# Key columns shared by neighbouring blocks: copied by DMA instead of ScalarE, with a new order of all work

## The chip, the cores and the metric

The kernel runs on one core of a Trainium2 chip. A core has a matrix engine (TensorE, PE in the profile; its weight loads are listed apart as PEld), a vector engine (VectorE, DVE), an activation engine (ScalarE, ACT), a general engine (GpSimd, POOL) and a sync engine (SyncE, SP), which in this kernel issues every DMA. Each engine works through its own list of instructions in order and waits on semaphores that the others, or a DMA that has landed, count up. PE writes its sums to PSUM; ACT and DVE copy ("evict") them from there to the on-chip memory SBUF.

The metric is the device time of one execution in microseconds. Lower is better. Before the change it was 191.21 us (median of 3 runs, 190.81 to 193.04).

## What is computed

One transformer layer in bfloat16 over 2048 positions of width 448: a sliding, dilated attention with 16 heads of width 28, and a shift-mixing MLP, each behind layer norms.

```python
def _A_ref(x, wqkv, wo):                      # attention
    H = 16; Dh = D // H; W, dil = 8, 2
    qkv = (x @ wqkv).reshape(B, S, 3, H, Dh)
    q, k, v = qkv[0], qkv[1], qkv[2]
    idx = pos[:, None] - off[None, :]         # off = 0, 2, 4, ..., 14
    logits = einsum("bhsd,bhswd->bhsw", q, kg) * Dh ** -0.5   # kg: k gathered at idx
    logits = where(idx >= 0, logits, -1e9)
    o = einsum("bhsw,bhswd->bhsd", softmax(logits), vg)
    return o.reshape(B, S, D) @ wo

def _B_ref(x, w1, w2, w3, w4):                # MLP
    h = gelu(layernorm(x) @ w1)
    # its four column quarters shifted by +1, -1, +2, -2 positions -> hs
    x1 = x + hs @ w2
    return x1 + gelu(layernorm(x1) @ w3) @ w4

h = x + _A_ref(layernorm(x), A_wqkv, A_wo)
return h + _B_ref(layernorm(h), B_w1, B_w2, B_w3, B_w4)
```

Position s attends to the keys s, s-2, ..., s-14. So a group of positions needs the 14 keys before its first one; the kernel keeps 16 columns (`PADK`) for them.

## The kernel before

**Blocks and phases.** The 2048 positions are 16 tiles of 128, and four blocks of 512 (t = 0 to 3). A block goes through these phases; a number behind the name is the block (M1 is phase M of block 1):

- N1: statistics and normalisation of the input x, tile by tile (DVE, ACT).
- A1: the normalised tiles are transposed (on PE for blocks 0 and 1, by a transposing DMA for blocks 2 and 3), then multiplied with the q and k columns of `wqkv`. Three chunks of 128 columns of q go to `qT`, three of k to `kk[t]`. The last 64 columns of each (the "half" chunk) are computed from their own weight copy `wr_s` and go to `qT[..., 3]` and `kr[t]`.
- V: the v product, evicted to `vt`; then SP copies it with overlaps into `vw` by three or four DMAs (the vw loads).
- A2 and S: for each chunk, DVE multiplies queries by eight shifted views of the keys (the "qk products", 128x4096, the half chunk 128x2048); PE sums over the head's rows; then the softmax, a handful of 128x512 steps on DVE and ACT, and a product into `pb` that can be done by DVE or POOL. PE turns `pb`, and ACT or DVE copies it to `pt[t]`.
- A3 and O: DVE spreads the weights with a mask into `bd` (four "mask products" a block, 80x2048), PE multiplies by `vw`, the result is copied to `actT`; then the product with `wo`, in two pairs of tiles, evicted to `xin` with the residual.
- B1 and M: statistics and normalisation of that, a transposing DMA (lntm to actT), the w1 product, gelu into `gT`.

The MLP's second part goes in five units of 2, 4, 4, 4 and 2 tiles (u = 0 to 4): B2 (the shifted w2 product, statistics), T (normalisation, transposing DMA), W3 (the w3 product and gelu; W30 is unit 0's) and B3 (the w4 product, the final sum, the store).

**Keys shared by blocks.** `kk[t]` holds 512 key columns behind 16 columns of the block before; phase A1 of block t fills those first 16 of block t+1 with an ACT copy (128x48 elements, SBUF to SBUF). `kr[t]` holds the half chunk's keys in eight groups of 64 positions, four on partitions 0 to 63 and four on 64 to 127, each group behind its own 16 columns; these are the last 16 columns of the group before, which lies on the other half of the partitions. Phase A1 evicts the half chunk's two PSUM banks (X and Y) with four ACT or DVE copies and then, with three more ACT copies from the same banks, fills the 16-column parts: 64x64, 64x48 and, for the next block, 64x16 elements. Lines 696 to 707 do this.

**What sets the order.** Each operation is recorded in a list and gets a number in the order of its creation. `ORDER` is a sequence of all these numbers; cut by engine, it is the order of each engine's list. `OTHER` names the operations that run on their second engine (`copy` has ACT first and DVE second; the `pb` product has DVE first and POOL second). `arrange` walks through the sequence, assigns buffers, and adds waits: a transposing DMA waits for all plain DMAs that stand between it and the transposing DMA before, and for that one; a plain DMA behind a transposing one waits for it:

```python
if op.insts[0][0] == "dma_start_transpose":
    op.deps.update(turned + moved)
    turned, moved = [op], []
elif op.is_dma and not callable(op.chan):
    op.deps.update(turned)
    moved.append(op)
```

ACT loads its function table anew (`emit_engine`) when it goes from exp and ln to gelu and back.

**The loads.** `load_rows` loads a weight matrix in two DMAs of two row chunks each; both have all 128 partitions. The input loads keep the order in which the code lists them: x tiles 0, 1, then 2 and 3, the q and k columns of `wqkv` (operations 12 and 13, 896 columns), x tiles 4 and 5 (14), 6 and 7 (15), the v columns (16, 17), the rest. All instructions are emitted from one helper, so nearly every row of the profile names line 986 (984 and 981 are its neighbours); they are told apart by their tiles and shapes.

Of the kernel before, what the change touches and what calls it, by code (L numbers as in the profile page):

```python
# [48 lines left out]
"""  # L49
OTHER = """  # L50
92 102 187 188 381 493 499 502 505 549 550
# [229 lines left out]
def bass_sequential_preLN__sliding_local_dilated__mixer_s_mlp__prompt_kernel(  # L281
    nc, A_x, A_wqkv, A_wo, B_x, B_w1, B_w2, B_w3, B_w4, out,
):
    _, SEQ, D = A_x.shape
# [26 lines left out]
    with ExitStack() as es:  # L311
# [118 lines left out]

        S.tag = "load"
# [4 lines left out]
        load_rows("wqk", wqkv_s[:, :, 0:2 * D], A_wqkv, 0, 2 * D)  # L436
# [231 lines left out]
        def phase_A1(t):  # L668
# [26 lines left out]

            def last(b, lo, n):
                return b(lambda v: v[64:128, 0:256].rearrange("p (j n) -> p j n", j=4)[:, lo:lo + n, 64 - PADK:])

            duo(half(X, 0, True), half(Y, 64, False), ((0, 256),))
            for h, b in enumerate((X, Y)):  # L700
                copy(qT[64 * h:64 * h + 64, 3, now:now + 256], b(lambda v: v[0:64, 0:256]))
# [3 lines left out]
            if t + 1 < NST:  # L705
                copy(kr[t + 1][0:64, 0:1, 0:PADK], last(Y, 3, 1), False)
                copy(kk[t + 1][:, :, 0:PADK], kk[t][:, :, 512:KVW])
# [320 lines left out]
```

## Time and profile before

| what | value |
|---|---|
| median of 3 runs | 191.21 us (190.81 to 193.04) |
| the profiled execution, its own time | 191.6 us |
| its span from first to last instruction | 189.9 us |
| granted TensorE clock | 1.00 throughout |
| DMA | 17.96 MB, 39.7% of 16 engines' span |
| SP waits before transposing DMAs for vw loads | 11.8 us, in 4 waits |

The span is what the trace covers; the 1.7 us around it belong to the execution's time too. A group's row reads: line, engine, operation, written tile, read tiles, shape and count, then busy us in all, mean ns of one, and the idle time just before with what ended it. A row of the timeline reads: start, duration, engine, line, operation, tiles, shape, count, and in brackets the idle time before it with what ended it. A row of the chain of waits reads: start, duration, what. A row of DMA issues reads: tiles, engine, kind, count, size of one, and the median us from issue to landing. In a row by stretch stand the stretch, its length, the busy time and count of PE, PEld, DVE, ACT and POOL, the granted clock, the busy share of the DMA engines and their GB/s.

Where the time lies, by the 40 slices of the page (each 4.75 us; a digit is a tenth of busy time, 9 is 90% or more):

```
PE   6799999999988668999999999999999999999994
DVE  6799999999999999897795337673973024001322
ACT  3569999999998999977698677049167004740330
```

### The profile page before, as it was taken

What the parts mean: (1) busy time and instruction counts of PE and PEld (TensorE: products, weight loads), DVE (VectorE), ACT (ScalarE), POOL (GpSimd) and SP (SyncE); (2) the same over time, 40 slices, a digit from 0 to 9 for tenths busy, and PEclk for the clock granted to TensorE, in tenths of its full rate; (3) what the DMA queues carried; (4) which work ended last, traced back from release to release, by engine and by line L of the source; (5) the groups of instructions that cost most, each with busy time, mean ns of one, the idle gap of its engine ahead of it and who ended that gap; (6) DMA issues with size and microseconds to landing.
All of it is one profiled execution on the core that took longest, in us unless ns stands there. A gap on an engine that the chain in (4) does not pass through costs nothing.

```text
span 189.9 us, 5626 instructions
## 1 busy us (share of the span) xinstructions
PE 178.4 (94%) x2434; PEld 107.5 (57%) x2434; DVE 127.4 (67%) x226; ACT 126.5 (67%) x295; POOL 26.9 (14%) x62
## 2 busy tenths in 40 slices
PE   6799989999988668999999999999999999999994
PEld 2494334545443434486544666666545664699973
DVE  6799999999999999897795337673973024001322
ACT  3569999999998999977698677049167004740330
POOL 2340000000002100202910000008026304000000
DMA  5993065554961553663534200518008202300202
GB/s 138 358 281 85 16 112 128 114 131 102 308 202 28 96 114 93 136 159 88 114 66 85 53 3 0 106 34 183 4 0 91 23 0 77 79 3 0 74 28 73
DMA packets 33217, 17.96 MB, mean 95 GB/s; under 512 B 21944, under 2 KB 32680, under 8 KB 33192
## 3 DMA queue, kind: packets, MB, share of 16 engines
q1 hardware_dynamic: 33192, 17.60, 39.7%
q8 instruction: 19, 0.31, 0.7%
q14 instruction: 6, 0.05, 0.1%
HBM read 7.91 MB, written 1.84 MB: 51 GB/s over the span
## 4 chain that ended last, share of the span: by engine, by line
PE 62%; DVE 17%; ACT 11%; DMA 6%; SPq 1%; issue 1%
PE ps L986 62%; DVE qk_r L986 9%; ACT arena L986 3%; DMA xin<-in_A_x_dram 3%; DMA actT<-lntm 3%; DVE bd_r L986 3%; ACT lntm L986 3%; ACT actT L986 2%; ACT vt L986 2%; DVE lntm L986 1%; DVE mx L986 1%; DVE st L986 1%; SPq L986 1%; ACT xin L986 1%; DVE pb L986 1%
## 5 line engine op out<-in xcount | busy, mean ns | idle before, releaser
L986 PE MATMUL ps<-actT,arena 64*128 64x512 bf16 (+1 forms) x756 | 68.8, 329 | 1.3 <-ACT vt L986 1.0
L986 PEld LDWEIGHTS ps<-actT,arena 64*128 64x128 bf16 x756 | 38.6, 94 | 27.3 <-ACT vt L986 2.6
L986 ACT ACTIVATE h3T<-ps 128x512 bf16<-128x512 f32 (+1 forms) x70 | 31.1, 515 | 33.7 <-PE ps L986 33.0
L986 PE MATMUL ps<-arena,h3T 64*128 64x448 bf16 (+2 forms) x434 | 44.5, 343 | 0.0
L986 PEld LDWEIGHTS ps<-arena,h3T 64*128 64x128 bf16 (+1 forms) x434 | 31.2, 94 | 11.5 <-ACT h3T L986 0.2
L986 DVE SCALAR_TENSOR_TENSOR qk_r<-ps,mrs,arena 128x448 bf16<-128x448 f32 (+1 forms) x17 | 10.6, 652 | 40.3 <-PE ps L986 33.2
L986 ACT ACTIVATE arena<-ps 128x512 bf16<-128x512 f32 (+6 forms) x73 | 32.8, 495 | 5.2 <-PE ps L986 4.6
L986 DVE TENSOR_TENSOR qk_r<-arena 128x4096 bf16<-128x4096 bf16 (+1 forms) x16 | 31.9, 2016 | 0.3 <-ACT arena L986 0.3
L986 POOL TENSOR_TENSOR arena<-arena,xin 128x448 f32<-128x448 f32 x16 | 16.7, 1066 | 43.5 <-DVE lntm L986 43.5
L986 DVE TENSOR_TENSOR bd_r<-arena,bmask 80x2048 bf16<-80x2048 bf16 x16 | 19.1, 1216 | 0.2 <-ACT arena L986 0.2
L986 PE MATMUL ps<-actT,w_s 64*112 64x512 bf16 x112 | 13.6, 378 | 2.2 <-DMA actT<-lntm 2.2
L986 PE MATMUL ps<-wo_s,actT 64*128 64x448 bf16 x128 | 14.8, 350 | 0.8 <-issue 0.5
L986 PE MATMUL ps<-w_s,arena 64*128 64x448 bf16 (+1 forms) x128 | 13.9, 350 | 1.0 <-ACT arena L986 1.0
L986 DVE SCALAR_TENSOR_TENSOR arena<-xin,rs_y,ps 128x448 f32<-128x448 bf16 x16 | 10.3, 676 | 4.0 <-PE ps L986 3.9
L986 PE MATMUL ps<-arena,actT 64*128 64x448 bf16 x112 | 12.5, 350 | 0.1
L986 ACT ACTIVATE lntm<-xin,nm 128x448 bf16<-128x448 bf16 x16 | 10.6, 685 | 2.2 <-DVE nm L986 2.0
L986 ACT ACTIVATE rs_x<-mv,epsilon 128x4 f32<-128x4 f32 (+2 forms) x16 | 4.9, 306 | 10.7 <-DVE mv L986 10.5
L986 ACT ACTIVATE actT<-ps 128x512 bf16<-128x512 f32 (+2 forms) x18 | 10.9, 644 | 1.4 <-PE ps L986 1.2
L986 PEld LDWEIGHTS ps<-actT,w_s 64*112 64x112 bf16 x112 | 7.7, 127 | 7.2 <-ACT arena L986 1.6
L986 PEld LDWEIGHTS ps<-w_s,arena 64*128 64x128 bf16 (+1 forms) x128 | 7.2, 94 | 6.1 <-ACT arena L986 1.1
L986 DVE BATCH_NORM_STATS2 st<-xin 128x6 f32<-128x448 bf16 x16 | 9.1, 616 | 1.7 <-DMA xin<-in_A_x_dram 1.4
L986 PEld LDWEIGHTS ps<-wo_s,actT 64*128 64x128 bf16 x128 | 6.2, 94 | 6.0 <-issue 0.9
(72 smaller groups left out, 156.6 us busy)
## 6 DMA issues: line engine op xcount, KB each, us to landing
arena<-in_B_w_dram SPq DMA_DIRECT2D x2, 896.0 KB, 8.1
out_dram<-qk_r SPq DMA_DIRECT2D x15, 112.0 KB, 1.9
arena<-in_B_w_dram SPq DMA_DIRECT2D x2, 784.0 KB, 5.2
vw<-vt SPq DMA_DIRECT2D x4, 320.0 KB, 5.7
vw<-vt SPq DMA_DIRECT2D x4, 256.0 KB, 3.9
arena<-in_A_wqkv_dram SPq DMA_DIRECT2D x2, 448.0 KB, 4.6
xin<-in_A_x_dram SPq DMA_DIRECT2D x2, 448.0 KB, 8.5
xin<-in_A_x_dram SPq DMA_DIRECT2D x3, 224.0 KB, 6.0
```

The costliest lines, as they stand in the source:

```text
L986: inst = getattr(eng, meth)(**kw)
```

## The change

Three edits.

1. The 16-column parts are no longer written by ACT. Where the four copies stood, four DMAs stand, which copy from the `kr[t]` and `kk[t]` that the other evictions have written, on SP's queue: `kra` (64 partitions x 4 groups x 16 columns, 8 KB), `krb` (6 KB), `krc` (2 KB, into the next block) and `kkp` (12 KB, into the next block). Block 3 has only the first two: 14 DMAs in all. `last`, which read the PSUM banks, is gone.
2. The q and k weights are loaded by `load_qk` in two column halves (columns 0 to 255 of q and of k, then 256 to 447), each with two DMAs for q and two for k: eight DMAs in place of two. Operation numbers from 14 on are therefore six higher.
3. `ORDER` and `OTHER` are new. `ORDER` has 864 numbers in place of 858. In the old numbering, `OTHER` no longer names the copy of tile 1's transpose (92), the eviction of chunk 0 of k (102), the norm of tile 1 in B1 (187), one A3 copy of block 3 (499) and one norm of unit 0 (549), so these run on ACT; it names the eviction of the half chunk of q from bank Y (119) for DVE and the `pb` product of block 3 for POOL, and of the two `pt` copies of block 3 the first in place of the second.

```diff
+        def load_qk(lo, n):
+
+            for g in range(2):
+                load_rows("wqk%d%d" % (lo, g), wqkv_s[:, :, g * D + lo:g * D + lo + n], A_wqkv, g * D + lo, n)
...
-        load_rows("wqk", wqkv_s[:, :, 0:2 * D], A_wqkv, 0, 2 * D)
+        for lo, n in ((0, 256), (256, D - 256)):
+            load_qk(lo, n)
...
-            def last(b, lo, n):
-                return b(lambda v: v[64:128, 0:256].rearrange("p (j n) -> p j n", j=4)[:, lo:lo + n, 64 - PADK:])
...
-            copy(kr[t][64:128, :, 0:PADK], last(X, 0, 4), False)
-            copy(kr[t][0:64, 1:4, 0:PADK], last(Y, 0, 3), False)
+            dma("kra%d" % t, kr[t][64:128, :, 0:PADK], kr[t][0:64, :, 64:KW], 64 * 4 * PADK * 2)
+            dma("krb%d" % t, kr[t][0:64, 1:4, 0:PADK], kr[t][64:128, 0:3, 64:KW], 64 * 3 * PADK * 2)
             if t + 1 < NST:
-                copy(kr[t + 1][0:64, 0:1, 0:PADK], last(Y, 3, 1), False)
-                copy(kk[t + 1][:, :, 0:PADK], kk[t][:, :, 512:KVW])
+                dma("krc%d" % t, kr[t + 1][0:64, 0, 0:PADK], kr[t][64:128, 3, 64:KW], 64 * PADK * 2)
+                dma("kkp%d" % t, kk[t + 1][:, :, 0:PADK], kk[t][:, :, 512:KVW], 128 * 3 * PADK * 2)
```

`OTHER` in the diff (new numbers, six higher):

```diff
-92 102 187 188 381 493 499 502 505 549 550
+125 194 387 496 498 508 511 556
```

What of the new order the prediction speaks of, in the new numbers, as the operations follow each other on one engine:

- DVE, start: statistics of x tiles 0 to 3, their norms, then the statistics of tiles 4 to 7 (205, 207, 209, 211), the norms of block 1, the statistics of block 2, the first qk product of block 0 (143), the norms of block 2, and the other three qk products of block 0. Before, three of block 0's products stood ahead of block 2's norms.
- SP: ..., transposing DMA of block 2's A1 (338), w1's second half, vw loads and `kr` copies of blocks 0 and 1, transposing DMA of block 3's A1 (449), a vw load, `kkp` of block 1 (246), vw loads and `kr` copies up to block 2, w2, w3, vw loads, B1's transposing DMA of block 0 (196), the vw load of 256 KB for block 2 (370), B1's transposing DMA of block 1 (315), `krb` of block 3, the first half of w4, ... Before, the load between the two transposing DMAs of B1 was one of 48 KB (366 in the old numbers).
- PE from O1 on: both pairs of O1 in order as their halves of A3 come, the first score chunk of block 3, the turn of block 2's `pb`, M0, all four A3 groups of block 2 with unit 0 of B2 between them, O2 and M1 mixed, unit 1 of B2, then W30. Before, two A3 groups of block 2 and the second pair of O2 (403, 404) stood behind M1, and that pair amid W30 and the w4 product of unit 0; the last score chunk of block 3 (489) stood ahead of W30 and now stands behind it.

58 rows, old and new, of the table ORDER are left out of this document.

## The prediction

> **What bounds the kernel now.** I read the page first, then the chain of waits in order of time.
>
> ```profile
> span 189.9 us, 5626 instructions
> ```
> ```profile
> 67.10 5.92 DMA actT<-lntm
> ...
> 73.07 35.45 PE ps L986 x583
> ...
> 108.60 78.75 PE ps L986 x820
> ```
>
> From 73.07 to 187.35 us the chain is PE alone (35.45 + 78.75), with 0.08 us between: the matrix work left at 73.07 fixes the rest. So a change gains only by getting PE through its early work sooner, or loses by opening holes later. The busy times by stretch (PE, PEld, DVE, ACT, POOL; then granted clock, DMA share, GB/s) say what bounds the early part:
>
> ```profile
> 5.00:10.00 5.00, 3.84 (x48) 2.50 (x48) 4.05 (x12) 2.54 (x8) 2.19 (x14) 1.00 1.05 359
> ...
> 15.00:20.00 5.00, 5.00 (x52) 2.17 (x50) 5.00 (x8) 5.00 (x14) 0.00 (x0) 1.00 0.19 43
> ...
> 55.00:60.00 5.00, 3.80 (x66) 1.61 (x66) 4.93 (x9) 4.97 (x14) 0.00 (x0) 1.00 0.13 32
> ```
>
> DVE and ACT are full from 15 us on; PE pays at the end of the attention part. The timeline of PE shows its holes there, in brackets:
>
> ```profile
> 56.35 0.42 PE L986 MATMUL ps<-bd_r,vw 80*32 80x64 bf16 x32 [0.38 <-DVE bd_r L986]
> 57.08 0.55 PE L986 MATMUL ps<-wo_s,actT 64*128 64x448 bf16 x4 [0.32 <-ACT actT L986]
> 58.14 0.55 PE L986 MATMUL ps<-wo_s,actT 64*128 64x448 bf16 x4 [0.51 <-issue]
> 64.39 3.23 PE L986 MATMUL ps<-actT,w_s 64*112 64x512 bf16 x28 [1.53 <-DMA actT<-lntm]
> 68.38 0.42 PE L986 MATMUL ps<-bd_r,vw 80*32 80x64 bf16 x32 [0.41 <-ACT arena L986]
> 69.75 1.93 PE L986 MATMUL ps<-w_s,arena 64*128 64x448 bf16 x16 [0.96 <-ACT arena L986]
> 73.07 3.23 PE L986 MATMUL ps<-actT,w_s 64*112 64x512 bf16 x28 [0.63 <-DMA actT<-lntm]
> ```
>
> They sum to 4.74 us. The two longest matmul rows are M0 and M1 (the w1 product of blocks 0 and 1), each waiting for its transposing DMA, which waits for the normalisation in phase B1.
>
> **Part one: work taken off ACT and DVE.** The copies that become DMAs, and operations that change engine:
>
> ```profile
> L986 ACT ACTIVATE arena<-ps 64x64 bf16<-64x64 f32 x4 | 0.9, 220 | 1.7 <-PE ps L986 1.7
> L986 ACT ACTIVATE arena<-ps 64x48 bf16<-64x48 f32 x4 | 0.8, 201 | 0.0
> L986 ACT ACTIVATE arena<-arena 128x48 bf16<-128x48 bf16 x3 | 0.8, 261 | 0.0
> L986 ACT ACTIVATE arena<-ps 64x16 bf16<-64x16 f32 x3 | 0.5, 181 | 0.1
> L986 ACT ACTIVATE actT<-ps 128x512 bf16<-128x512 bf16 x3 | 1.6, 597 | 0.5 <-PE ps L986 0.5
> L986 ACT ACTIVATE arena<-ps 128x512 bf16<-128x512 f32 x23 | 13.0, 618 | 0.0
> L986 ACT ACTIVATE lntm<-xin,nmr,rs_y 128x512 bf16<-128x512 bf16 x2 | 1.5, 799 | 0.0
> L986 DVE COPY actT<-ps 128x512 bf16<-128x512 bf16 x1 | 0.4, 418 | 0.0
> L986 DVE CAST arena<-ps 128x512 bf16<-128x512 f32 x1 | 0.7, 657 | 0.0
> L986 DVE TENSOR_SCALAR lntm<-xin,nm,rs_y 128x512 bf16<-128x512 bf16 x14 | 5.1, 407 | 0.4 <-ACT rs_y L986 0.3
> L986 ACT ACTIVATE arena<-ps 64x256 bf16<-64x256 f32 x16 | 6.0, 375 | 0.3
> ```
>
> ACT loses 14 small copies: 0.9 + 0.8 + 0.8 + 0.5 = 3.0 us, all before 73 us. But OTHER changes too. Three operations that DVE ran in the first two blocks go back to ACT (597 + 618 + 799 ns = 2.0 us) and save DVE 418 + 657 + 407 = 1.48 us; one 64x256 eviction goes from ACT (0.38) to DVE, where no row shows it: between 0.33 (half the 128x512 CAST, 657 ns) and 0.66 (all of it), and I take 0.4, half its elements plus something fixed. Net in front: ACT -3.0 + 2.0 - 0.4 = -1.4 us, DVE -1.1 (-0.8 to -1.15). The other moves (one softmax product to POOL, two evictions back to ACT) are of block 3 or the MLP, under the full PE, and cost nothing unless PE runs dry.
>
> **Part two: the loads.** Two q/k loads become eight.
>
> ```profile
> 2.20 0.98 SPq L986 DMA_DIRECT2D arena<-in_A_wqkv_dram  x2
> 3.22 1.07 SPq L986 DMA_DIRECT2D xin<-in_A_x_dram  x2
> 9.27 2.21 DVE L986 BATCH_NORM_STATS2 st<-xin 128x6 f32<-128x448 bf16 x4 [0.91 <-DMA xin<-in_A_x_dram]
> ```
>
> One issue is 0.98/2 = 0.49 us, so six more push the next load, x of tiles 4 and 5, from 3.22 to 6.14. DVE already waits 0.91 us for it and has nothing else in its order. It was 6.0 us under way (3.22 to 9.27) while the DMA engines moved 359 GB/s: it stood in a bandwidth queue behind the same weights, so it need not land 2.9 us later. Ends: 0 and 2.9; I take 0.5, near the queued row. On the other side the first q/k piece needs only the first column half and its first two tiles are evicted earlier, about half a microsecond for PE, which is not the bound there. I count that at nothing and expect this start to eat DVE's saving: even at 25 us.
>
> **Part three: the new DMAs on SP.** 14 copies of 16 columns enter SP's queue, each behind an ACT eviction, and each is ahead of what follows there.
>
> ```profile
> vw<-vt SPq DMA_DIRECT2D x4, 256.0 KB, 3.9
> ...
> vw<-vt SPq DMA_DIRECT2D x4, 48.0 KB, 2.6
> ...
> out_dram<-qk_r SPq DMA_DIRECT2D x2, 56.0 KB, 1.5
> vw<-vt SPq DMA_DIRECT2D x3, 16.0 KB, 5.2
> ```
> ```profile
> L986 DVE TENSOR_TENSOR qk_r<-arena 128x4096 bf16<-128x4096 bf16 x12 | 27.1, 2282 | 0.3 <-ACT arena L986 0.3
> ...
> L986 DVE TENSOR_TENSOR bd_r<-arena,bmask 80x2048 bf16<-80x2048 bf16 x16 | 19.1, 1216 | 0.2 <-ACT arena L986 0.2
> ```
>
> The nearest in size land in 1.5 to 5.2 us; I take 2.6, SBUF to SBUF. Plain and transposing DMAs wait for each other in the plan, so a copy queued behind a transpose waits for it. Who waits is a DVE product. The copies for blocks 0, 1 and 3 have over 4 us of DVE work in between. The tightest is block 2's first 16 keys (246 in the new numbering): it stands behind block 3's transpose (449) and one vw load, and product 377 reads it. Between the norms that feed 449 and that product DVE's order holds one and a half qk products (2.28 each), four mask products (1.22) and five softmax steps (priced as the CAST, 0.66): 11.6 us. Against it stand the transpose (4.5 to 5.9, from 59.90 to 64.39 and from the chain), two issues (0.63 each, below) and 2.6 to land: 8.4 to 9.8. Landing in 5.2 makes 12.4 and a stall of 0.8. I take none.
>
> **Part four: the order.** Here the gain must come.
>
> ```profile
> 59.90 2.12 SPq L986 DMA_TRANSPOSE actT<-lntm  x1
> ...
> 64.27 0.63 SPq L986 DMA_DIRECT2D vw<-vt  x1
> ...
> 89.89 2.04 SPq L986 DMA_TRANSPOSE actT<-lntm  x1
> ```
> ```profile
> 81.95 5.19 PE L986 MATMUL ps<-actT,arena 64*128 64x256 bf16 x92
> 86.97 0.92 PE L986 MATMUL ps<-wo_s,actT 64*128 64x448 bf16 x8
> ...
> 94.41 10.09 PE L986 MATMUL ps<-actT,arena 64*128 64x512 bf16 x92
> ```
>
> M0's transpose (before: 59.90): ACT now has 13 of the copies (2.8 us) and a few evictions less ahead of the last norm, so it can leave at about 57; M0 then waits instead for O1 (56.35 to 58.14 show it begin), whose last mask product now stands behind two softmax steps and a norm (0.66 + 0.66 + 0.41 = 1.7 us). M0 starts near 62, not 64.39.
>
> M1's transpose (67.10): O1's pairs now finish one after the other, two of the four statistics early; the last norm ends about 65.7. But a 256 KB vw load is now queued between the two transposes where a 48 KB one was (64.27): it goes out as M0 starts, so it lands at 62 + 0.6 + 3.9 = 66.5. With 4.5 to 5.9 for the transpose, M1 starts near 71.6, 1.5 us earlier.
>
> From M1 to W30 (first w3 product) PE took 81.95 - 73.07 = 8.88 us. The new order has both late O2 sums in there (0.92 each) and three short groups (about 0.42 each) elsewhere: 8.88 + 1.84 - 1.26 = 9.5, plus 0.8 of waiting for M1's last gelu: W30 at 81.9. That is the old time with 1.84 - 0.42 = 1.4 us more work done. The next turn (89.89) then limits: W31 has 1.8 us less to hide it and the statistics end only about 1 us sooner, so I take 1.3 us to the end. The later order still interleaves w1, w3 and w4 products with every transpose; I count no new hole.
>
> **The sum.** Span 189.9 - 1.3 = 188.6. The profiled execution's own time was 191.6, 1.7 above its span, so 190.3; the median of the runs was 191.2, 0.4 below that, which makes 189.9.
>
> **Rivals.**
> *ACT was the bound.* If the 2.8 us freed on ACT pass through and all 4.74 us of holes close: 191.2 - 4.7 = 186.5. For: ACT at 4.97 of 5 from 55 to 60. Against: DVE is at 5.00 longer, and gains 1.1.
> *The x load comes late.* If tiles 4 and 5 keep their 6.0 us, they land at 12.2; every full DVE stretch moves by 2.9: 189.9 + 2.9 = 192.8, slower than before as soon as they land more than 1.3 us after 9.27. Against: 359 GB/s. The Trainium skill ("DMA: Bandwidth & Descriptors", Specifications) says that runs under 512 B fall short of line rate through read-modify-write; the second half's runs are 192 columns, 384 B, and no row here shows such a load. Were its 393 KB to take twice their time at 359 GB/s, my estimate by that page is 1.1 us more, 193.9.
> *SP becomes the bound.* In-order copies behind transposes keep DVE idle before a product in blocks 1 to 3. Two misses of 2.0 to 2.6 us give 189.9 + 4.6 = 194.5, and one more 196 to 197. For: SP has 20 issues more, and the mutual waits of copies and transposes. Deciding point: 246 landing after DVE reaches 377.
> *It does nothing.* The time earned at M1 is given back at W31's turn: 191.2.
>
> **How the numbers follow.** Forecast (188.5 to 190.9) 0.37; nothing 0.13; ACT bound 0.18; late x 0.14; SP 0.18. The range reaches from the first rival's 186.5 to 195.0, which takes in the late load and over half of the SP case. 2% (3.8 us) is about what a measurement of this kernel tells from no change: faster means under 187.4, slower over 195.0. Faster gets the ACT rival, 0.18; slower the larger half of the SP rival and a little of the late load, 0.17; the rest, 0.65, is within.
>
> **What would show it.** Right: no DVE idle from the x load above 1.5 us; the ACT groups 64x64, 64x48, 64x16 and 128x48 gone; M0's matmuls near 62, M1's near 71.6; PE holes between 55 and 75 of 3 to 3.5 us; the last chain PE alone from there. Wrong: a qk product whose releaser is a DMA into the arena; M1 at 73 or later; a PE hole before W30 or W31 longer than 1 us; or first statistics of block 1 after 10.6.

## The result: a little slower, and the profile after

| | before | changed |
|---|---|---|
| median (22 runs each, side by side) | 191.63 us | 192.30 us |
| ratio, 95% interval | | 1.0049 (1.0025 to 1.0073) |
| span of the profiled execution | 189.9 us | 190.8 us |
| M0, M1, W30 start at | 64.39, 73.07, 81.95 | 64.50, 73.29, 83.22 |
| PE busy, DVE, ACT, POOL (us) | 178.4, 127.4, 126.5, 26.9 | 180.0, 128.6, 123.3, 30.9 |

The change makes the kernel 0.5% slower. Some executions of either kernel run in a slower state; every ratio here leaves those out, so 1.0049 is not 192.30/191.63. Helper rows name line 989 now (986 before, others in the kernels of the experiments), 984 is ACT's table load. The chain of waits of the changed kernel (start, duration, what) no longer goes over to PE alone at M1:

```profile
67.87 5.37 DMA actT<-lntm
73.29 6.39 PE ps L989 x60
...
87.21 2.77 DVE lntm L989 x4
...
98.35 1.09 ACT h3T L989 x2
...
103.27 84.26 PE ps L989 x989
```

PE alone begins 30 us later than before (103.27; before 73.07): between M1 and there the chain runs through DVE's norms of unit 1 and ACT. PE's timeline shows the holes that are left, and a new one:

```profile
59.56 0.42 PE L989 MATMUL ps<-bd_r,vw 80*32 80x64 bf16 x32 [0.66 <-DVE bd_r L989]
60.71 0.93 PE L989 MATMUL ps<-wo_s,actT 64*128 64x448 bf16 x8 [0.73 <-ACT actT L989]
64.50 3.23 PE L989 MATMUL ps<-actT,w_s 64*112 64x512 bf16 x28 [0.52 <-ACT vt L989]
...
73.29 1.07 PE L989 MATMUL ps<-actT,w_s 64*112 64x512 bf16 x8 [0.58 <-DMA actT<-lntm]
83.22 5.53 PE L989 MATMUL ps<-actT,arena 64*128 64x256 bf16 x98 [0.21 <-DVE mv L989]
...
97.03 5.75 PE L989 MATMUL ps<-actT,arena 64*128 64x512 bf16 x48
103.26 2.58 PE L989 MATMUL ps<-actT,w_s 64*112 64x512 bf16 x22 [0.47 <-ACT h3T L989]
```

PE's holes between 55 and 75 us sum to 3.20 us (4.74 before). The row at 103.26 is M2's first part, behind W31; it waits 0.47 us, and from W30 to there 20.04 us pass, which p4 below does in 19.14. Before, PE had no hole there. The row names a gelu of ACT (h3T) as what ended the wait, but M2 also needs block 2's transposing DMA, and that came no sooner: it left at 98.78, SP's next DMA, which waits for it, went out at 103.14, and M2's first weight load started at 103.22. In p4 the three times are 97.52, 101.86 and 101.95, and M2 does not wait. DVE's timeline shows the start and this stage:

```profile
10.11 1.68 DVE L989 BATCH_NORM_STATS2 st<-xin 128x6 f32<-128x448 bf16 x3 [2.10 <-DMA xin<-in_A_x_dram]
...
16.83 2.26 DVE L989 TENSOR_TENSOR qk_r<-arena 128x4096 bf16<-128x4096 bf16 x1
...
87.21 2.77 DVE L989 TENSOR_SCALAR lntm<-arena,mv,rs_y 128x512 bf16<-128x512 f32 x4 [1.07 <-POOL rs_y L989]
...
96.65 2.10 DVE L989 TENSOR_SCALAR lntm<-xin,nm,rs_y 128x512 bf16<-128x512 bf16 x4 [0.65 <-ACT rs_y L989]
...
99.38 6.42 DVE L989 TENSOR_TENSOR bd_r<-arena,bmask 80x2048 bf16<-80x2048 bf16 x4
```

In the kernel before, the same norms of unit 1 and two of the mask products were

```profile
87.90 1.92 DVE L986 TENSOR_SCALAR lntm<-arena,mv,rs_y 128x512 bf16<-128x512 f32 x4 [1.14 <-POOL rs_y L986]
...
97.15 2.35 DVE L986 TENSOR_TENSOR bd_r<-arena,bmask 80x2048 bf16<-80x2048 bf16 x2
```

So two things stand out: DVE waits 2.10 us for the x of tiles 4 and 5 (0.91 before) and begins its first qk product at 16.83 (15.98); and the same DVE operations take longer in the stage of W31 (four norms 2.77 for 1.92, mask products 1.6 each for 1.2). It is single instructions that stretch: one of unit 1's four norms takes 1.40 us where the median is 0.54, one of block 2's four takes 1.12 where it is 0.41, and the transposing DMA of M2 waits for the latter. POOL's timeline tells what ran beside them:

```profile
87.29 1.04 POOL L989 TENSOR_TENSOR arena<-arena,xin 128x448 f32<-128x448 f32 x1
...
97.40 4.21 POOL L989 TENSOR_TENSOR arena<-arena,xin 128x448 f32<-128x448 f32 x3
```

These are the additions of unit 0's and unit 1's residual. One takes 1.04 us beside the norms and 1.40 beside the mask products (1.01 late in the kernel, where three take 3.02).

### The profile page after: what moved, and what is told of

The parts are those of the page before. It is cut to its first block, busy times and chain, and to the rows that moved or that the text cites. A ratio compares the mean times of both kernels' runs of the same rounds, so it can differ in the third digit from the quotient of the medians.

```text
span 190.8 us, 5638 instructions
## 1 busy us (share of the span) xinstructions
PE 180.0 (94%) x2434; PEld 100.1 (52%) x2434; DVE 128.6 (67%) x221; ACT 123.3 (65%) x283; POOL 30.9 (16%) x63
## 4 chain that ended last, share of the span: by engine, by line
PE 51%; DVE 24%; ACT 15%; DMA 5%; SPq 3%; issue 1%; POOL 1%
PE ps L989 51%; DVE qk_r L989 8%; ACT arena L989 4%; DVE bd_r L989 4%; DVE st L989 3%; DVE lntm L989 3%; DMA actT<-lntm 3%; SPq L989 3%; ACT lntm L989 3%; DMA xin<-in_A_x_dram 2%; DVE mx L989 2%; DVE arena L989 1%; ACT actT L989 1%; ACT xin L989 1%; ACT h3T L989 1%
## 5 line engine op out<-in xcount | busy, mean ns | idle before, releaser
L989 PEld LDWEIGHTS ps<-actT,arena 64*128 64x128 bf16 x756 | 37.6, 94 | 28.5 <-POOL arena L989 1.3
L989 ACT ACTIVATE arena<-ps 128x512 bf16<-128x512 f32 (+3 forms) x62 | 31.2, 551 | 5.1 <-PE ps L989 4.7
L989 PEld LDWEIGHTS ps<-arena,h3T 64*128 64x128 bf16 (+1 forms) x434 | 24.6, 94 | 17.1 <-PE ps L989 0.2
L989 POOL TENSOR_TENSOR arena<-arena,xin 128x448 f32<-128x448 f32 x16 | 18.5, 1180 | 35.3 <-DVE lntm L989 19.9
L989 DVE TENSOR_TENSOR bd_r<-arena,bmask 80x2048 bf16<-80x2048 bf16 x16 | 20.8, 1327 | 0.2 <-ACT arena L989 0.2
L989 ACT ACTIVATE actT<-ps 128x512 bf16<-128x512 f32 (+2 forms) x20 | 12.3, 640 | 5.0 <-PE ps L989 5.0
L989 PE MATMUL ps<-wo_s,actT 64*128 64x448 bf16 x128 | 14.3, 350 | 0.9 <-ACT actT L989 0.7
L989 POOL TENSOR_TENSOR pb<-ls,mx 128x512 bf16<-128x512 f32 x2 | 2.9, 1426 | 56.1 <-ACT mx L989 56.1
L989 PEld LDWEIGHTS ps<-w_s,arena 64*128 64x128 bf16 (+1 forms) x128 | 6.6, 95 | 6.3 <-PE ps L989 0.9
L989 DVE TENSOR_SCALAR lntm<-arena,mv,rs_y 128x512 bf16<-128x512 f32 x14 | 7.7, 602 | 2.8 <-POOL rs_y L989 2.2
```

The lines of the kernel that those rows point to most:

```text
L989: inst = getattr(eng, meth)(**kw)
```

## The experiments

Theories at the start: (T1) the loss is the late x at the start and the hole behind W31, and the copies by DMA are harmless; (T2) the copies by DMA and SP's queue are the cost; (T3) ACT, or DVE, was the only bound, so that relief of the other is worth nothing. Each kernel was compared with the kernel before on the same chip; a ratio is to that.

**l1: the two whole weight loads again.**

```diff
-        for lo, n in ((0, 256), (256, D - 256)):
-            load_qk(lo, n)
+        load_rows("wqk", wqkv_s[:, :, 0:2 * D], A_wqkv, 0, 2 * D)
```

> The changed kernel, with the q and k weights loaded in the two whole transfers of before; the searched order and the copies by DMA stay. My theory: the eight issues put the x of tiles 4 and 5 on their way 3.1 us later than before, and DVE and PE carry 0.75 us of it (first product of q and k at 16.83 instead of 15.98). Undone, this stage gains 0.6 to 0.9 us, and if the gain is kept to the end the ratio to before is 1.000 to 1.002 (1.005 for the whole change). The rival, that a stage later on takes the time whatever reaches it: the first product comes earlier, M0 and M1 do not, and the ratio stays at 1.004 to 1.006. A second rival, that the order was searched for the late weights: ratio over 1.006.

Ratio 0.9974 (0.9945 to 1.0004), span 189.7. DVE's and PE's timelines of l1:

```profile
8.67 1.68 DVE L995 BATCH_NORM_STATS2 st<-xin 128x6 f32<-128x448 bf16 x3 [0.66 <-DMA xin<-in_A_x_dram]
...
15.44 2.26 DVE L995 TENSOR_TENSOR qk_r<-arena 128x4096 bf16<-128x4096 bf16 x1
```
```profile
63.20 3.23 PE L995 MATMUL ps<-actT,w_s 64*112 64x512 bf16 x28 [0.35 <-DMA actT<-lntm]
...
102.20 2.58 PE L995 MATMUL ps<-actT,w_s 64*112 64x512 bf16 x22 [0.47 <-ACT h3T L995]
```

Against the changed kernel the first product moves by 1.39 us, M0 by 1.30, the hole behind W31 by 1.06, the span by 1.1: what the start loses arrives at the end nearly whole, more than my 0.75. The hole behind W31 stays, as it must if it has a cause of its own. The ratio lies below what I expected (1.000 to 1.002).

**h1: the old order behind W30.**

```diff
-ORDER: the new one, 864 numbers
+ORDER: its first 482 numbers, then the rest in the order of the kernel before
```

> The changed kernel up to the first product of W30, in its own order (482 operations); every operation behind it in the order that the kernel before gives it. My theory: the hole of about 1.0 us in W31 (103.26, waiting for a gelu of ACT) belongs to the new order of the back part, so it goes, and the ratio falls to 0.998 to 1.001. The rival, that ACT cannot serve W31 earlier whatever the order, since its work up to there (S3, B12 and two table loads) hangs on DVE: the hole stays under another name and the ratio stays at 1.003 to 1.006.

Block 3's `pb` product and two of its copies also go back to their engines of before. Ratio 1.0219 (1.0165 to 1.0272): neither. PE's timeline:

```profile
85.78 0.40 PE L996 MATMUL ps<-qk_r,zc 128*32 128x512 bf16 x4 [3.22 <-DVE qk_r L996]
```

The old order has block 3's last score chunk ahead of W30, and the new one's DVE has not made its product by then. The splice makes its own hole, and the run says nothing on the hole behind W31.

**c2 and c3: the copies back on ACT,** c2 with the eight loads, c3 with two.

```diff
-            dma("kra%d" % t, kr[t][64:128, :, 0:PADK], kr[t][0:64, :, 64:KW], 64 * 4 * PADK * 2)
+            copy(kr[t][64:128, :, 0:PADK], last(X, 0, 4), False)
```

(and the other three likewise)

> The changed kernel, its order and its two column halves kept, with the 14 copies done by ACT again, each right behind the eviction of the same bank. If ACT sets the front (worth 3.0 us of its time less the 0.2 to 0.4 us that issuing costs elsewhere), the ratio rises from 1.005 to 1.013 to 1.020. My theory, that DVE sets it and ACT has room there: under 0.5 us more, 1.004 to 1.008. The rival that the transfers hurt (a queue on SP, a late wait): below 1.003.

> The new order alone: two whole weight loads, and the 14 copies done by ACT right behind the eviction of their bank. If the three parts of the change add up (eight loads +0.75%, copies by DMA -0.55%, whole change +0.49%), the order alone gives 1.002 to 1.004. The rival, that the order was worth something only together with the copies by DMA, or the loads cost less without them: above 1.006 or below 1.000.

c2: 1.0104 (1.0069 to 1.0139), M0 at 65.57 and M1 at 74.12, 1.07 and 0.83 us later than in the changed kernel. c3: 1.0036 (1.0018 to 1.0053). So the copies by DMA are worth 0.0055 (c2 against the changed kernel) and 0.0062 (c3 against l1) of the time, about 1.1 us of the 3.0 us that ACT loses: between the two sides of c2's expectation. DVE's timeline of c2 shows how ACT's work reaches DVE:

```profile
32.41 1.38 DVE L999 TENSOR_SCALAR lntm<-xin,nm,rs_y 128x512 bf16<-128x512 bf16 x4 [0.35 <-ACT rs_y L999]
...
44.70 0.69 DVE L999 TENSOR_REDUCE mx<-ls 128x64 f32<-128x512 f32 x1 [0.60 <-ACT ls L999]
```

Up to M0, DVE's waits for ACT sum to 1.71 us in c2 and 0.64 in the changed kernel, and the difference is the 1.07 us by which M0 is late. Neither engine alone is the bound, each waits for the other for moments (T3 falls), and the copies earn their place (T2 falls for this order). c3 is the new order by itself: it costs 0.36% before the copies earn anything.

**n1: the kernel before with the eight loads.**

```diff
-        load_rows("wqk", wqkv_s[:, :, 0:2 * D], A_wqkv, 0, 2 * D)
+        for lo, n in ((0, 256), (256, D - 256)):
+            load_qk(lo, n)
```

> The kernel before, with its order and its copies on ACT; only the q and k weights come in eight loads. My theory: the x of tiles 4 and 5 comes 1.2 to 1.5 us later and everything behind it moves by that: ratio 1.005 to 1.008, first product of q and k at 17.0 to 17.5. The rival, that only the new order, which does all statistics of block 1 at once, is exposed to the late x: 0.999 to 1.003.

1.0023 (0.9991 to 1.0054): by the ratio the rival's, by the first product (17.11) the theory's. DVE's timeline:

```profile
9.79 2.20 DVE L999 BATCH_NORM_STATS2 st<-xin 128x6 f32<-128x448 bf16 x4 [1.75 <-DMA xin<-in_A_x_dram]
14.71 2.20 DVE L999 BATCH_NORM_STATS2 st<-xin 128x6 f32<-128x448 bf16 x4 [0.51 <-DMA xin<-in_A_x_dram]
17.11 4.46 DVE L999 TENSOR_TENSOR qk_r<-arena 128x4096 bf16<-128x4096 bf16 x2
```

The x comes 0.5 us later than before (9.79; before 9.27), DVE waits for a second load too, the first product is 1.13 us late; M0 then is 0.67 us late (65.06). The old order absorbs half of it; the new one next to none (l1: 1.39 us at the first product, 1.30 at M0).

**l2 and l3: x ahead of the second column halves,** tiles 4 and 5 in l2, 4 to 7 in l3.

```diff
-        for lo, n in ((0, 256), (256, D - 256)):
-            load_qk(lo, n)
+        load_qk(0, 256)
         load_x(4, 2)
+        load_qk(256, D - 256)
         load_x(6, 2)
```

> The changed kernel with its eight loads, but the x of tiles 4 and 5 issued behind the fourth of them, ahead of the second column halves. My theory (the x issued late is the cost, the halves themselves are not): x lands near 8.7 as with two loads, ratio 0.996 to 0.999. The rival, that the halves cost by themselves (runs of 384 and 512 bytes, second halves on which PE then waits): PE waits over 1.5 us for the half chunk's weights or the second halves, ratio 1.002 to 1.006.

> The changed kernel with its eight loads, the x of tiles 4 to 7 issued behind the fourth of them, ahead of the second column halves. With tiles 4 and 5 alone ahead, the wait moved to tile 6 (1.59 us at 10.68). My theory, that the wait is a matter of place in the queue: no wait of DVE for x above 0.5 us now, but the second halves come last, and PE waits for the half chunk's weights 2 us or more (1.61 with two tiles ahead); the first product of q and k at 15.0 to 16.3, ratio 0.998 to 1.003. The rival, that six more loads cost little and only the x was late: PE's wait stays under 1.7 us and the ratio falls to 0.995 to 0.998.

l2: 1.0028 (0.9985 to 1.0070), as the rival has it; l3: 1.0125 (1.0077 to 1.0173), slower than both of its theories. In l2 no wait for tiles 4 and 5 is left, but tile 6 is waited for, and PE for the second halves, by way of POOL, which copies the half chunk's weights; DVE's and PE's rows:

```profile
10.68 0.63 DVE L996 BATCH_NORM_STATS2 st<-xin 128x6 f32<-128x448 bf16 x1 [1.59 <-DMA xin<-in_A_x_dram]
```
```profile
10.46 4.32 PE L996 MATMUL ps<-actT,arena 64*128 64x256 bf16 x76 [1.61 <-POOL arena L996]
```

In l3 DVE waits 0.29 us for x, but PE 2.74 us, up to 11.52, for the half chunk's weights, and the first product starts at 18.85. Each place in the queue that one load gains another loses: what is late is the whole queue.

**l4: four loads with whole rows.**

```diff
-        for lo, n in ((0, 256), (256, D - 256)):
-            load_qk(lo, n)
+        load_qk(0, D)
```

> The changed kernel with four q and k loads: two for all columns of q, two for all columns of k (runs of 896 bytes in place of 512 and 384). From 4 to 10 us the DMA engines moved 235 GB/s in the changed kernel at a busy share of 0.91, and 340 at 1.04 with the two loads of before. If the short runs cost, the rate is over 300 GB/s here, the x of tiles 4 and 5 lands before 9.0, the first product of q and k starts at 15.2 to 15.8: ratio 0.995 to 0.999. If the number of issues costs, half of it is left: x at 9.2 to 9.6, first product at 16.0 to 16.4, ratio 1.000 to 1.003.

0.9994 (0.9964 to 1.0024). x of tiles 4 and 5 is issued at 4.25 (3.22 in l1, 6.29 in the changed kernel) and read at 9.35 (8.67, 10.11); the first product starts at 16.10, as the theory of issues has it. The rate recovers as the theory of short runs has it. The stretch from 4 to 10 us (busy times of PE, PEld, DVE, ACT, POOL, then clock, DMA share, GB/s) of the kernel before, the changed one and l4:

```profile
4.00:10.00 6.00, 4.84 (x50) 2.85 (x50) 4.86 (x14) 2.93 (x10) 2.19 (x14) 1.00 1.04 357
```
```profile
4.00:10.00 6.00, 5.01 (x42) 2.61 (x42) 3.57 (x12) 3.41 (x10) 1.05 (x5) 1.00 0.91 235
```
```profile
4.00:10.00 6.00, 5.14 (x44) 2.93 (x44) 4.34 (x14) 3.56 (x10) 1.21 (x5) 1.00 1.02 327
```

SP's rows show one limit: eight issues take 4.05 us, 0.506 each, for 128 KB in the first half and 96 KB in the second. 131 thousand bytes in 0.506 us are 259 GB/s, 98 thousand 194, and SP asks for no more while it issues them; before, the DMA engines moved 357:

```profile
2.20 4.05 SPq L989 DMA_DIRECT2D arena<-in_A_wqkv_dram  x8
6.29 0.98 SPq L989 DMA_DIRECT2D xin<-in_A_x_dram  x2
```

But that limit is the smaller part. Behind the last of the eight issues, from 6.25 to 9 us, the rate is still 228 GB/s at a busy share of 0.93 (before 348 at 1.04), though larger loads are queued by then. Over the whole stretch the busy share fell by an eighth (0.91 for 1.04) and the bytes by a third, so a busy engine moved fewer bytes too. The shorter runs fit that, but they were not tested alone: l4 lengthens the runs and doubles the bytes of an issue together.

**p1, p2, p3, p4: POOL's additions moved.** POOL's list and, in p2, DVE's, PE's and SP's places of the last score chunk (numbers of the kernel before; 551 is unit 0's second addition, 612, 614 and 615 are unit 1's, 607 is a power in unit 1's norms):

```diff
-l1:     552 607 185 551 490 88 414 614 615 612 304
+p1, p2: 552 551 607 185 490 88 414 614 615 612 304
+p3:     552 551 607 614 615 612 185 490 88 414 304
-DVE l1: 606 299 609 610 611 608 405 482 484
+DVE p2: 606 482 299 609 610 611 608 405 484
-PE l1:  582 583 483 584
+PE p2:  582 483 583 584
```

p4 is the changed kernel itself, eight loads included, with p3's list on POOL.

> The changed kernel with two whole weight loads (ratio 0.9974 by itself), and four residual additions of POOL moved: that of unit 0 behind the one ahead of it, three of unit 1 behind the last mask product of block 3. My theory: DVE runs slower beside a POOL addition (unit 1's norms 2.77 us for four where the kernel before shows 1.92; mask products 1.6 us each there, 1.22 elsewhere). With the additions away the norms take about 1.95 and the mask products about 1.25 each, and the hole behind W31 shrinks by 0.2 to 0.5 us: ratio 0.994 to 0.997. The rival, that their length comes from something else (their operands, the port of PSUM, ACT beside them): the same lengths and 0.997 to 0.999.

> As p1, and the last score chunk of block 3 earlier: its query-key product on DVE in the 1.07 us in which DVE waits for POOL ahead of unit 1's norms (87.21 in the changed kernel), its matmuls between the first and second half of unit 0's first w4 sum. My theory: ACT's list is what starts W31's gelus late (98.35), and the score chunk's softmax steps stand in it ahead of them; the chain of that softmax starts 1.0 to 1.4 us sooner, the hole behind W31 closes: ratio 0.991 to 0.994. The rival, that the statistics of block 2 in the same list or PE's own queue set it: 0.995 to 0.998, with the hole at the same place.

> As p1 (two whole weight loads, unit 0's addition early), but the three POOL additions of unit 1 now stand directly behind that unit's norms, in the 7 us in which POOL waits; in p1 nothing stood between them and the place where they ran before, so they ran there again (97.02 to 101.2), and DVE's mask products beside them still took 6.42 us for four. If POOL's additions slow DVE, the mask products fall to about 4.9 us for four and block 2's norms from 2.10 to about 1.4; M2 (waiting for its transposing DMA in p1) comes 0.5 to 0.8 us sooner behind W30: ratio 0.988 to 0.994. The rival, that the length of these products is their own: 6.4 us again, and p1's time.

> The changed kernel as it is, eight loads included; only POOL's residual additions of units 0 and 1 stand earlier in POOL's list, as in p3. My theory: those additions beside DVE's norms and mask products are what opens the hole behind W31 (1.0 us), so it goes, and the ratio falls from 1.005 to 0.998 to 1.001; the start stays late (first product of q and k at 16.8). The rival, that ACT's list or the table loads open the hole: it stays, 1.003 to 1.006.

Ratios: p1 0.9898 (0.9840 to 0.9957), p2 0.9966 (0.9935 to 0.9998), p3 0.9922 (0.9885 to 0.9959), p4 0.9959 (0.9933 to 0.9985). p1 and p4 are faster than their theories, p3 as its own, p2 as its rival. In p1 only unit 0's addition really moved. The norms beside it went back to 1.91 us; the hole behind W31 stayed, now in the name of a transposing DMA (102.85, 0.44 us), and the additions of unit 1 still ran at 97.02 beside block 2's norms (2.10) and the mask products (6.42). p3 moves those too; DVE's and PE's rows, from its timelines:

```profile
85.64 1.92 DVE L995 TENSOR_SCALAR lntm<-arena,mv,rs_y 128x512 bf16<-128x512 f32 x4 [1.07 <-POOL rs_y L995]
...
94.93 1.38 DVE L995 TENSOR_SCALAR lntm<-xin,nm,rs_y 128x512 bf16<-128x512 bf16 x4 [0.61 <-ACT rs_y L995]
...
96.94 1.34 DVE L995 TENSOR_TENSOR bd_r<-arena,bmask 80x2048 bf16<-80x2048 bf16 x1
98.71 3.49 DVE L995 TENSOR_TENSOR bd_r<-arena,bmask 80x2048 bf16<-80x2048 bf16 x3 [0.43 <-ACT arena L995]
```
```profile
81.74 5.53 PE L995 MATMUL ps<-actT,arena 64*128 64x256 bf16 x98 [0.30 <-DVE mv L995]
```

The lengths fall to what they are without POOL (mask products 4.83 for 6.42 in all; the first, 1.34, still has an addition beside it), and the second fence has PE's last hole: behind 81.74 it never waits. In p4 the start is late as ever (first product at 17.11), but PE's timeline and the end of the chain are

```profile
82.94 5.51 PE L996 MATMUL ps<-actT,arena 64*128 64x256 bf16 x98
...
102.08 2.54 PE L996 MATMUL ps<-actT,w_s 64*112 64x512 bf16 x22
```
```profile
73.37 112.94 PE ps L996 x1333
```

with PE alone from M1 on, as before the change.

This is the changed kernel with four instructions of POOL elsewhere in its list, ACT's list untouched, and it is faster than before. So ACT's list did not open the hole, though the profile names ACT there, and my theory of p2 fell. With l1 and p3 this bears out T1: the late x and the hole behind W31 are the loss, and without both the kernel is faster than before. In p2 itself the score chunk's product waited 2.06 us for a copy by DMA, unit 1's norms behind it came 2 us later, its exponential started no sooner (93.60; 93.47 in the changed kernel), and PE got a new hole of 0.80 us at 94.50. p1 and p3 cannot be told apart by their ratios.

**q2 and q3: w4 behind unit 0's transposing DMA.** SP's list:

```diff
-p3: 309 463 537 553 538 462 616
+q2: 309 463 553 537 538 462 616
+q3: 309 463 462 553 537 538 616
```

(537 and 538 are w4's halves, 553 and 616 the transposing DMAs of units 0 and 1, 462 and 463 block 3's copies)

> As p3, and the first half of w4 issued behind unit 0's transposing DMA, not ahead of it. In the changed kernel SP waits 8.0 us in two waits for weight loads before transposing DMAs; unit 0's leaves at 79.94 and lands at 83.1, where W30 starts (83.22). My theory: this load, not DVE's statistics, sets W30 in some executions (p1's profile: 1.37 us of hole there); with the load behind, the transposing DMA leaves at 77 to 78, W30 starts without a hole, ratio 0.1 to 0.5% below p3. The rival: w4 then lands too late for unit 0's first w4 sum, which starts about 5 us behind W30; hole of 0.5 us and more there, ratio at or above p3.

> As q2 (two loads, additions early, first half of w4 behind unit 0's transposing DMA), and block 3's copy of the half chunk's keys issued ahead of that transposing DMA instead of behind both halves of w4, where it took 7.1 us to land and held the last score chunk's product. My theory: no hole before W30 and none at the score chunk; 0.986 to 0.991. The rival: w4 lands too late for unit 0's first w4 sum, hole of 0.5 us or more there, 0.990 to 0.994.

q2: 0.9920 (0.9892 to 0.9949); q3: 0.9947 (0.9910 to 0.9984). The transposing DMA leaves at 76.25 and 76.59 (78.40 in p3) and W30's hole (0.30 us in p3, 1.37 in p1) is gone, but each pays it back. From the chain of q2, then of q3:

```profile
80.89 7.11 DMA arena<-arena
88.02 1.91 DVE qk_r L995
89.97 95.28 PE ps L995 x1107
```
```profile
80.67 7.69 DMA arena<-in_B_w_dram
88.49 96.71 PE ps L995 x1121
```

In q2 an 8 KB copy behind 1.6 MB of weights takes 7.11 us to land, and PE waits 1.35 us for the product that reads it; in q3 w4 itself comes 0.85 us too late, as the rival has it. Neither gains over p3.

**c1, c1b, c1c: the copies by DMA alone, in the old order.** SP's list (237 to 240, 351 to 354, 462 and 463 are the copies; 443, 190 and 309 transposing DMAs):

```diff
-c1:  237 238 239 134 443 240 351 252 354 251 352 353 250 364 26 363 27 28 365 190 463 366 462 309 537
+c1b: 134 237 238 443 239 240 252 251 250 364 26 351 352 363 354 27 28 365 190 463 366 353 462 309 537
+c1c: 134 237 238 443 239 240 252 251 250 364 26 351 352 363 354 27 28 365 190 366 309 463 462 353 537
```

> The kernel before, with its order and its two whole weight transfers; only the 14 copies go by DMA, each at its old place in the order or right behind the eviction that it reads. ACT loses 3.0 us. If ACT sets the front: ratio 0.985 to 0.992. My theory, DVE sets it: 0.997 to 1.001. The rival that transfers between the blocks cost through SP's queue or through a late wait: 1.003 to 1.010, with a product of q and k, or a transpose, that starts later and names a transfer as its releaser.

> As c1 (the kernel before, copies by DMA), with the copies at other places of SP's queue: a vw load and block 3's transposing DMA go ahead of copies of block 1, and block 2's copies go behind the vw loads and w2. If c1's loss is made in the queue (a copy that waits for its eviction holds up the loads and transposing DMAs behind it, the weights come 6 us later and meet a vw load), most of it goes: 0.998 to 1.012. The rival, that the copies land too late for their readers wherever they stand: over 1.025, with products that name a DMA into the arena as what they waited for.

> As c1b, and the three copies that block 3's half chunk still needs go behind the transposing DMA of block 1's MLP. If the queue explains the loss, that transposing DMA leaves near 67 to 69 again, M1 starts at 73 to 75, and the ratio falls from 1.034 to 1.000 to 1.012. The rival, that the copies cost in another way: over 1.02.

Ratios 1.0457 (1.0404 to 1.0511), 1.0344 (1.0294 to 1.0394), 1.0162 (1.0095 to 1.0228). c1 is slower than even its rival; c1b has its rival's ratio, but no DVE product in it names a copy as what it waited for. SP stands at a copy until its eviction is done. In c1 the loads of w3 behind such copies went out at 52.63 (before 46.15), met a vw load, and M0's transposing DMA, which waits for that, left at 63.94 (before 59.90). c1b's chain shows the next place, ahead of M1:

```profile
71.49 0.38 ACT arena L990
71.90 1.83 DMA arena<-arena
73.74 4.34 DMA actT<-lntm
78.13 116.47 PE ps L990 x1404
```

The copy waits for an eviction of ACT, the transposing DMA for the copy, and leaves at 73.74 (before 67.10). The copies moved to later places give back 2.95 of the 4.57 points, step by step. c1c misses its upper end (1.012): the transposing DMA of block 1 leaves at 69.39, yet PE has a hole of 2.34 us between O1's first products (up to 59.07; 0.51 there before), with no releaser in the trace. What of the 1.6% comes from there stays open. Part of all three losses is PE's granted clock, which falls in them and not in the changed kernel (last section).

## Why the prediction was wrong

**The frame** was right as far as it went: what is lost early arrives at the end (l1). That nothing would be lost behind M1 was an assumption, and it failed: with the two old loads, moving POOL's additions alone takes the span from 189.7 us (l1) to 188.4 (p3). The miss of 2.2 us has two parts of about the same size: the loads (1.1 us of span) and the new hole (1.3). Of the signs that would show the prediction wrong, M1 at 73 or later came true; DVE's wait for x (2.10 us) was above the 1.5 that would show it right.

**Part one** (ACT -1.4 us, DVE -1.1) has no time of its own in the sum, which takes its 1.3 us from the order. The copies by DMA alone are worth 0.55 to 0.62% (about 1.1 us), so the gain was real; it comes from ACT, through DVE's short waits for it (c2).

**Part two** failed in the size of its term: "it stood in a bandwidth queue behind the same weights, so it need not land 2.9 us later ... I take 0.5". Against the old loads in the same order the first product starts 1.39 us later (l1), inside the bounds of 0 and 2.9 but well above what I took; the loads cost 0.68 to 0.75% in the new order (0.37% with POOL's additions moved). "Even at 25 us" was 0.85 us behind at the first product already (16.83, then 15.98). The queue was real, but I held its rate fixed, and the change lowers it, from 357 to 235 GB/s. The Trainium skill ("DMA: Bandwidth & Descriptors", Specifications) has runs under 512 B below line rate; the trace has 220 packets under 512 B in the first 14 us before and 1327 after (1297 in n1, where the loads are the only difference), and fewer bytes for the same busy time, which agrees; SP's half microsecond an issue comes on top. My rival of the late load was right in kind and had 0.14; it said 192.8, from a full 2.9 us. The factor of two behind its 193.9 was a supposition, which the page does not give: from 4 to 10 us a busy engine moved 258 GB/s for 343 (235/0.91 and 357/1.04).

**Part three** held in the order that was measured: no qk product waited for a copy. The landing time was mis-sized (2.6 taken; medians of 2.4 to 4.0 by size in the changed kernel, 7.11 in q2). The rival that SP's queue becomes the bound is a true mechanism: with the same copies the old order is 1.6 to 4.6% slower. In the new order as it was measured it does not happen (p2 shows how near it is).

**Part four.** M0 was to start near 62, M1 at 71.6, W30 at 81.9; they came at 64.50, 73.29 and 83.22, and in l1, without the late start, at 63.20, 72.23 and 81.80. So W30's term was right but for part two, and partly by luck: in l1 M0 came 1.2 us and M1 0.6 us later than forecast, and the 0.8 us of waiting that the sum counts ahead of W30 was not there. The second step that failed, beside part two's 0.5 us, is the last one of part four: "the later order still interleaves w1, w3 and w4 products with every transpose; I count no new hole". There is one, of about 1 us, and p4 shows its cause by taking it away: four residual additions that the new order leaves on POOL beside DVE's norms and mask products, so that block 2's transposing DMA leaves late and M2 waits for it. I looked at PE, DVE, ACT and SP in the new order and not at what POOL does beside DVE. The Trainium skill ("SBUF — State Buffer", Who interferes with whom) says that VectorE and GpSimd share a pair of memory ports, and that a VectorE instruction with two inputs in SBUF, or one in a faster two-port mode, and a GpSimd instruction that reads SBUF block each other. The trace agrees: four norms 1.92 to 2.77 us, with all of the difference in one of them, mask products 1.2 to 1.6 each on average, POOL's additions 1.01 to 1.40 and one of 2.01. That they get longer together, and short again apart, the runs show; that the ports are the reason is the page's word.

**The sum.** 188.6 us of span was forecast, 190.8 measured. With both mis-sized terms taken out (two loads, POOL's additions moved), p3 has 188.4 and a ratio of 0.9922: faster than both kernels. So the sign was wrong by two terms of about 1 us each.

The parts as measured, each against the kernel that lacks only it (each difference between two runs is uncertain by about 0.4 points, so +0.37 and -0.52 are hardly clear of nothing):

| part | change of the ratio, points |
|---|---|
| new order alone (c3) | +0.36 (0.18 to 0.53) |
| copies by DMA, in the new order | -0.55, -0.62 |
| eight loads, in the new order | +0.75, +0.68; with POOL moved +0.37 |
| eight loads, in the old order (n1) | +0.23 (-0.09 to +0.54) |
| POOL's additions moved | -0.90 (eight loads), -0.52 (two) |

## What to carry to other kernels

When a load is cut into more pieces with shorter runs, compare the rate of the DMA engines, and their rate for the same busy share, before and after; where it falls, everything behind the load in the queue comes late. The bytes of one issue over the time of one issue give a second limit. When an order changes, look at which POOL and DVE instructions now run at the same time, even if neither is the bound: here both got longer, and the trace showed it as a slower row and not as a wait, with the wait that it caused put down to a third engine. A small copy on an in-order DMA queue costs what it holds up behind it and what is queued ahead of it, not its bytes.

## What the runs showed of the hardware that was not expected

In the experiments in which PE stood still or worked little for 2 to 4 us, its granted clock fell to 0.50, and the next products paid. PE busy and the granted clock (behind POOL's column) by stretch in c1b, where a hole of 2.67 us ends at 78.13:

```profile
70.00:74.00 4.00, 2.85 (x54) 1.31 (x52) 3.34 (x3) 3.94 (x8) 0.00 (x0) 0.85 0.05 6
74.00:78.00 4.00, 1.46 (x8) 0.31 (x4) 3.93 (x8) 3.34 (x10) 0.00 (x0) 0.50 0.68 131
78.00:82.00 4.00, 3.87 (x18) 1.99 (x20) 1.94 (x3) 0.81 (x1) 1.03 (x1) 0.50 0.64 197
```
```profile
78.13 5.64 PE L990 MATMUL ps<-actT,w_s 64*112 64x512 bf16 x28 [2.67 <-DMA actT<-lntm]
```

M1's 28 products (the second fence, PE's timeline) took 5.64 us there and 3.23 before. The hole of 2.67 us did not bring the clock down: by single microseconds it was 1.00 up to 72, 0.90 in the next and 0.50 from 73 to 83, and the hole lies between 75.46 and 78.13. What lies ahead of the fall are holes of 0.94 and 0.96 us, with PE busy for 1.98 of the 4 us from 68 to 72. c1c falls for some 3 us behind a hole of 2.34 us, and again behind two of 1.13 and 0.95, h1 behind one of 3.22; the holes of the kernel before, up to 1.53 us, leave the clock at 1.00 in its profiled execution. The Trainium skill ("TensorE: Matmul & The Clock Gate", Part 1) gives one idle window of about 3.4 us as what halves the clock; in c1b, c1c and h1 no hole was that long, and in c1b two of about 0.95 us, among little work, were enough.

Copies of 2 to 12 KB inside the on-chip memory took 2.4 to 4.0 us to land (medians by size in the changed kernel), about as long as a vw load of 256 KB (3.5).
